# Attention sinks of eight heads turned and multiplied as one, and the inverse sums' transposes placed later

## The chip, the cores and the metric

The kernel runs on one core of a Trainium2 chip. The metric is device time in microseconds (us) of one execution, as the median of three runs. A core has five engines that work side by side, each through its own list of instructions in order: TensorE (PE in the profile; its weight loads are listed apart as PEld), VectorE (DVE), ScalarE (ACT), GpSimd (POOL) and SyncE (SP), which here only issues DMAs.

## The reference

Windowed attention with sinks is followed by two MoE-like layers:

```python
scores = scale * np.matmul(q, k.transpose(0, 1, 3, 2))      # q, k, v: 2 x 8 heads x 768 x 64
keep = (pos[None, :] < n_sink) | ((rel >= 0) & (rel < window))   # n_sink 4, window 128
a = softmax(np.where(keep, scores, -1e9))
x = np.matmul(a, v)                                          # -> 1536 tokens x 512
x = (g1(x @ w_in1)) @ w_out1                                 # 512 -> 2048 -> 512, g1(h) = h * tanh(softplus(h))
out = (g2(x @ w_in2)) @ w_out2                               # the same shape, g2(h) = h * clip(h + 3, 0, 6) / 6
```

The weights arrive as 64-bit numbers and are decoded on the chip.

## The kernel before, in words

The sequence of each of the two batches is cut into six units of 128 queries, with all eight heads in a unit. Eight units are computed early, in full float32, before and beside the first MoE matmuls: 6 and 7 (the second batch's first two) and 0 to 5 (the first batch), in the order 6, 7, 0, 1, 2, 3, 4, 5. The other four are computed later by other functions. Tokens go through the MoE in three blocks; the first block needs units 6, 7, 0 and 1, the second 2 to 5.

A query of a unit sees the keys of its own unit and of the one before. From the third unit of a batch on (i > 1, the early units 2 to 5) the sinks, keys 0 to 15, lie outside these, so each head has a third segment of 16 columns: scores are 128 x 272 a head (128 + 128 + 16). An early unit goes through these steps of the class `First`, where g is one of two halves of four heads:

- `prep`: keys and queries are turned by TensorE and copied by ScalarE; GpSimd puts the 16 sink keys behind the unit's keys (line 331).
- `scores(g)`: score matmuls (350), VectorE adds the mask and takes the extreme (354), ScalarE takes the exponential and its row sum (358).
- `turn(g)`: the exponentials `d` are transposed by TensorE (369) and copied to `at` by ScalarE or VectorE (371, 373). If i > 1, VectorE gathers the sink columns of four heads into `ds`, 128 x 64 (377), TensorE turns it (379), VectorE copies it to `ats`, 64 x 128 (380).
- `values(g)`: for i > 1 first one sink matmul for each pair of heads, over 64 rows, four heads by 16 sinks (388), and then the window's matmuls (393), all into the unit's one PSUM tile `o`.
- `inverse`: VectorE takes the reciprocal of the row sums (401, 402), GpSimd spreads it over 128 x 512 as `rb` (405), TensorE turns `rb` in four transposes (407), and ScalarE copies the result to `rib` (409).
- `normalise`: VectorE multiplies `o` by `rib` (413). `outputs` splits the product into two halves of 16 bits (419, 420).

`first_blocks` emits the steps of neighbouring units interleaved. The emission order is not quite the order of execution: a planner lays out the instructions of each engine by priority and by its own forecast of times, so that weight decoding (lines 210 to 224), emitted later, stands in gaps of VectorE and ScalarE. Transposes of attention and the MoE's accumulators share four PSUM banks (`ps_acc`), scores, `o` and the MoE's hidden layer four others (`ps_h`).

The sink values are laid out once for a batch in `first_sinks`: 16 sinks of each head are loaded as 64 rows for each half by two DMAs (303). GpSimd multiplies the rows by a column of `selh` for each of four head places (306), which leaves a block matrix `vsb`, so that one matmul adds each head's own sinks. `selh` is the sum of two column sets, `a` for rows 0 to 63 and `b_` for rows 64 to 127, made by VectorE (149 to 153).

The MoE stages are steps of an up-projection (lines 737 to 739) and a down-projection (782), the second one step behind. VectorE's line 754 makes the down-projection's input.

Of the kernel before, what the change touches and what calls it, by code (L numbers as in the profile page):

```python
# [7 lines left out]
F32 = mybir.dt.float32  # L8
# [4 lines left out]
ALU = mybir.AluOpType  # L13
# [16 lines left out]
def attention_moe_moe2(  # L30
# [13 lines left out]
    nc = tc.nc  # L44
    B, H, S, D = q.shape
# [6 lines left out]
    HP = H // 2  # L52
# [6 lines left out]
    const = main.enter_context(tc.tile_pool(name="const", bufs=1))  # L59
# [7 lines left out]
    ps_acc = main.enter_context(tc.tile_pool(name="ps_acc", bufs=4, space=PSUM))  # L67
# [20 lines left out]
    m1, m2 = m_all[:, 0:256], m_all[:, 128:400]  # L88
    m0 = const.tile([128, 128], F32)
    selh = const.tile([128, 4], F32)  # L90
    ident = const.tile([128, 128], F32)
    nsw = keep.tile([128, 2], F32)

# [28 lines left out]
    def emit_masks():  # L122
        ns, wd = nsw[:, 0:1], nsw[:, 1:2]
        tmp = part_p.tile([128, 4, 128], F32, tag="part", name="tmp")
        col, rel, ind, dg = (tmp[:, i] for i in range(4))
        nc.gpsimd.iota(col, pattern=[[1, 128]], base=0, channel_multiplier=0, allow_small_or_imprecise_dtypes=True)
        nc.gpsimd.iota(rel, pattern=[[-1, 128]], base=0, channel_multiplier=1, allow_small_or_imprecise_dtypes=True)
        nc.vector.tensor_scalar(out=ident, in0=rel, scalar1=0.0, scalar2=None, op0=ALU.is_equal)

        nc.vector.tensor_scalar(out=ind, in0=rel, scalar1=0.0, scalar2=None, op0=ALU.is_ge)  # L130
        nc.vector.scalar_tensor_tensor(out=dg, in0=rel, scalar=wd, in1=ind, op0=ALU.is_lt, op1=ALU.mult)
        nc.vector.tensor_scalar(out=m2[:, 0:128], in0=dg, scalar1=-BIG, scalar2=BIG, op0=ALU.mult, op1=ALU.add)

        nc.vector.scalar_tensor_tensor(out=ind, in0=col, scalar=ns, in1=dg, op0=ALU.is_lt, op1=ALU.max)
        nc.vector.tensor_scalar(out=m0, in0=ind, scalar1=-BIG, scalar2=BIG, op0=ALU.mult, op1=ALU.add)

        nc.vector.tensor_scalar(out=ind[:, 0:16], in0=col[:, 0:16], scalar1=ns, scalar2=None, op0=ALU.is_lt)
        nc.vector.tensor_scalar(out=m2[:, 256:272], in0=ind[:, 0:16], scalar1=-BIG, scalar2=BIG, op0=ALU.mult, op1=ALU.add)

        nc.vector.tensor_scalar(out=dg, in0=rel, scalar1=128.0, scalar2=wd, op0=ALU.add, op1=ALU.is_lt)  # L140
        nc.vector.tensor_scalar(out=m2[:, 128:256], in0=dg, scalar1=-BIG, scalar2=BIG, op0=ALU.mult, op1=ALU.add)
        nc.vector.scalar_tensor_tensor(out=ind, in0=col, scalar=ns, in1=dg, op0=ALU.is_lt, op1=ALU.max)
        nc.vector.tensor_scalar(out=m1[:, 0:128], in0=ind, scalar1=-BIG, scalar2=BIG, op0=ALU.mult, op1=ALU.add)

        hp = const.tile([128, 4], F32)
        nc.gpsimd.iota(hp, pattern=[[-16, 4]], base=0, channel_multiplier=1, allow_small_or_imprecise_dtypes=True)
        a = const.tile([128, 4], F32)
        b_ = const.tile([128, 4], F32)
        nc.vector.tensor_scalar(out=a, in0=hp, scalar1=0.0, scalar2=None, op0=ALU.is_ge)
        nc.vector.scalar_tensor_tensor(out=a, in0=hp, scalar=16.0, in1=a, op0=ALU.is_lt, op1=ALU.mult)  # L150
        nc.vector.tensor_scalar(out=b_, in0=hp, scalar1=64.0, scalar2=None, op0=ALU.is_ge)
        nc.vector.scalar_tensor_tensor(out=b_, in0=hp, scalar=80.0, in1=b_, op0=ALU.is_lt, op1=ALU.mult)
        nc.vector.tensor_tensor(out=selh, in0=a, in1=b_, op=ALU.add)
# [131 lines left out]
    sink_n = {}  # L285
# [10 lines left out]
    def first_sinks(b):  # L296


        ks1 = c_p.tile([128, HP, 16], F32, name=f"ks1_{b}")
        nc.scalar.activation(out=ks1, in_=kv_n[b * NSB][0][:, :, 0:16], func=AF.Copy)  # L300
        vsn = c_p.tile([64, 2, D], F32, name=f"vsn_{b}")
        for g in range(2):
            nc.sync.dma_start(out=vsn[:, g, :], in_=v[b, 4 * g:4 * g + 4, 0:16, :])
        vsb = c_p.tile([64, 2, 4, D], F32, name=f"vsb_{b}")
        for h in range(4):
            nc.gpsimd.tensor_scalar(out=vsb[:, :, h, :], in0=vsn, scalar1=selh[0:64, h:h + 1], scalar2=None, op0=ALU.mult)
        sink_n[b] = (ks1, vsb)

    class First:
        def __init__(self, u):  # L310
            self.u = u
            self.b, self.i = divmod(u, NSB)
            self.d, self.at, self.ats = [None, None], [None, None], [None, None]

        def prep(self, pin=False):
            u, b, i = self.u, self.b, self.i
# [46 lines left out]
        def turn(self, g):  # L363
            d = self.d[g]
            at = self.at[g] = v_p.tile([128, 2, 4, 128], F32, tag="at", name="at")
            for m in range(len(self.kvs)):
                tp = ps_acc.tile([128, 4, 128], F32, tag="acc", name="tp")
                for hh in range(4):
                    nc.tensor.transpose(tp[:, hh, :], d[:, hh, m * 128:(m + 1) * 128], ident)
                if m <= g:  # L370
                    nc.scalar.activation(out=at[:, m], in_=tp, func=AF.Copy)
                else:
                    nc.vector.tensor_copy(out=at[:, m], in_=tp)
            if self.i > 1:
                ats = self.ats[g] = s_p.tile([64, 128], F32, tag="ats", name="ats")
                ds = s_p.tile([128, 4, 16], F32, tag="ds", name="ds")
                nc.vector.tensor_copy(out=ds, in_=d[:, :, 256:272])
                tp = ps_acc.tile([64, 128], F32, tag="acc", name="tp")
                nc.tensor.transpose(tp, ds.rearrange("p h s -> p (h s)"), ident)
                nc.vector.tensor_copy(out=ats, in_=tp)  # L380

        def values(self, g):
            if g == 0:
                self.o = ps_h.tile([128, HP, 128], F32, tag="h", name="o")
            if self.i > 1:
                for c in (2 * g, 2 * g + 1):
                    vsb = sink_n[self.b][1][:, g, 2 * (c % 2):2 * (c % 2) + 2].rearrange("p h d -> p (h d)")
                    nc.tensor.matmul(self.o[:, c, :], vsb, self.ats[g], start=c == 0, stop=False, skip_group_check=True)
            for c in (2 * g, 2 * g + 1):
                for m, kv in enumerate(self.kvs):  # L390
                    for r in range(2):
                        h = 2 * c + r
                        nc.tensor.matmul(  # L393
                            self.o[64 * r:64 * r + 64, c, :], kv[1][:, h, :], self.at[g][:, m, h % 4, :],
                            start=self.i <= 1 and c == 0 and m == 0, stop=c == HP - 1 and m == len(self.kvs) - 1, skip_group_check=True,
                        )

        def inverse(self):
            rs = s_p.tile([128, H], F32, tag="rs", name="rs")
            ri = s_p.tile([128, H, 1], F32, tag="ri", name="ri")  # L400
            nc.vector.tensor_scalar(out=rs, in0=self.sums, scalar1=1e-9, scalar2=2.0 ** -SX, op0=ALU.add, op1=ALU.mult)
            nc.vector.reciprocal(out=ri[:, :, 0], in_=rs)
            tp = ps_acc.tile([128, HP, 128], F32, tag="acc", name="tp")
            rb = b_p.tile([128, H, D], F32, tag="rb", name="rb")
            nc.gpsimd.tensor_copy(out=rb, in_=ri.to_broadcast([128, H, D]))
            for c in range(HP):
                nc.tensor.transpose(tp[:, c, :], rb[:, 2 * c:2 * c + 2, :].rearrange("p a d -> p (a d)"), ident)
            self.rib = rib = b_p.tile([128, HP, 128], F32, tag="rib", name="rib")
            nc.scalar.activation(out=rib, in_=tp, func=AF.Copy)
# [14 lines left out]
    def first_blocks():  # L424
# [7 lines left out]
        for n, e in enumerate(us):  # L432
            f = us[n + 1] if n + 1 < len(us) else None
            if n + 4 < len(us):
                load_first(first[n + 4])
            e.turn(0)
            if f:
                f.scores(0)
            if f is None:
                next(moe)  # L440
            if n > 0:
                us[n - 1].outputs()
            e.values(0)
            if n + 2 < len(us):
                us[n + 2].prep()
            e.inverse()
            e.turn(1)
            if f:
                f.scores(1)
            if n == len(us) - 2:  # L450
                next(moe)
            e.values(1)
            e.normalise()
# [263 lines left out]
    acc = {}  # L717
# [504 lines left out]
```

## Time and profile before

| | |
|---|---|
| median of 3 runs | 600.29 us (599.73 to 600.51) |
| profiled execution | 599.53 us, of which the span of the instructions is 597.7 us |
| TensorE matmul busy | 579.0 us, 97% |
| TensorE weight loads busy | 394.4 us, 66% |
| VectorE busy | 457.8 us, 77% |
| ScalarE busy | 398.4 us, 67% |
| GpSimd busy | 24.8 us, 4% |

The busy time of an engine is the part of the span in which an instruction ran on it. The ends of matmuls are modelled and neighbouring ones overlap, so a busy TensorE can still be a waiting one. An average over the span also hides that stages have different limits; views of single stretches show these. A chain of work is followed back from the last instruction, at each step to what released it.

### The profile page before, as it was taken

The page shows a single profiled execution, that of the slowest core. Times are in us where ns is not written, and L with a number is a line of the kernel's source. Part 1 is how long each engine was busy: PE and PEld are TensorE (multiplying, and loading weights), DVE is VectorE, ACT ScalarE, POOL GpSimd, SP SyncE. Part 2 cuts the span into 40 slices and gives each one's busy share as a digit, 9 for nine tenths or more (in the row PEclk, how much of TensorE's full clock was granted, in tenths as well). Part 3 has the DMA queues.
Part 4 walks back from the last instruction along what each step waited for, and adds up shares of the span by engine and source line. Part 5 has one row for each costly group of instructions (what it writes and reads, how often), then busy time and mean ns, then how long its engine had stood idle before and what let it go on. Part 6 is the DMA issues. An engine that isn't in the chain of part 4 may idle for free.

```text
span 597.7 us, 11394 instructions
## 1 busy us (share of the span) xinstructions
PE 579.0 (97%) x4430; PEld 394.4 (66%) x4430; DVE 457.8 (77%) x1102; ACT 398.4 (67%) x786; POOL 24.8 (4%) x36
## 2 busy tenths in 40 slices
PE   7999999999999999899989999999999999999996
PEld 4778754444444545444434468888888888888885
DVE  5688998999365555489999999866687889874754
ACT  5998887777687776679888887434354656553532
POOL 0040010700000000000000000000000000000000
PEclk9999999999999999999999999999999999999999
DMA  9976357998334533254453442000007676400001
GB/s 179 226 163 212 101 183 199 230 261 213 96 73 74 80 60 73 47 159 141 157 192 122 163 143 71 1 1 2 1 7 249 215 263 223 142 34 1 36 1 39
DMA packets 105842, 72.24 MB, mean 121 GB/s; under 512 B 73512, under 2 KB 98088, under 8 KB 105784
## 3 DMA queue, kind: packets, MB, share of 16 engines
q1 hardware_dynamic: 105784, 71.48, 42.9%
q8 instruction: 35, 0.57, 0.4%
q14 instruction: 23, 0.19, 0.1%
HBM read 60.43 MB, written 3.15 MB: 106 GB/s over the span
## 4 chain that ended last, share of the span: by engine, by line
PE 59%; DVE 13%; ACT 12%; issue 11%; DMA 2%; POOL 2%; SPq 1%; DVEq 0%; ACTq 0%
PE acc L846 18%; PE h L806 7%; PE h L808 7%; PE h L807 7%; PE acc L782 6%; PE h L737 3%; PE h L739 2%; PE h L738 2%; DVE p L212 2%; ACT e L745 2%; ACT e L746 2%; DVE g L754 2%; ACT d L358 2%; ACT y L215 1%; PE o L393 1%
## 5 line engine op out<-in xcount | busy, mean ns | idle before, releaser
L782 PE MATMUL acc<-g,w 128*128 128x512 f16 x576 | 131.2, 379 | 5.4 <-DVE g L754 5.1
L846 PE MATMUL acc<-w,g 128*128 128x256 f16 x1008 | 113.8, 273 | 0.0
L846 PEld LDWEIGHTS <-g 128*128 128x128 f16 x1008 | 98.6, 98 | 11.4
L806 PE MATMUL h<-xt,w 128*128 128x256 f16 x384 | 104.7, 273 | 0.0
L808 PE MATMUL h<-xt,w 128*128 128x256 f16 x384 | 104.7, 273 | 0.0
L807 PE MATMUL h<-xt,w 128*128 128x256 f16 x384 | 104.7, 273 | 0.0
L782 PEld LDWEIGHTS <-w 128*128 128x128 f16 x576 | 55.3, 98 | 71.6 <-issue 7.0
L737 PE MATMUL h<-xt,w 128*128 128x512 f16 x192 | 72.8, 379 | 1.8 <-DVE mins L558 1.2
L739 PE MATMUL h<-xt,w 128*128 128x512 f16 x192 | 72.8, 379 | 0.0
L738 PE MATMUL h<-xt,w 128*128 128x512 f16 x192 | 72.8, 379 | 0.0
L810 ACT ACTIVATE e<-h,bias 128x512 f32<-128x512 f32 x48 | 32.5, 678 | 54.5 <-PE h L808 54.5
L811 DVE SCALAR_TENSOR_TENSOR e<-e,h 128x512 f32<-128x512 f32 x48 | 32.8, 684 | 41.8 <-ACT e L810 41.8
L823 ACT ACTIVATE g<-e 128x256 f16<-128x256 f32 x96 | 29.5, 354 | 28.8 <-DVE e L811 28.8
L823 ACT ACTIVATE g<-sm 128x512 f16<-128x512 f32 x48 | 30.2, 628 | 27.5 <-DVE sm L818 27.5
L749 DVE SCALAR_TENSOR_TENSOR e<-e,h 128x512 f32<-128x512 f32 x48 | 30.8, 683 | 16.5 <-ACT e L747 16.3
L824 DVE SCALAR_TENSOR_TENSOR g<-sm,g 128x512 f16<-128x512 f32 x48 | 33.1, 689 | 10.9 <-ACT g L823 10.8
L806 PEld LDWEIGHTS <-w 128*128 128x128 f16 x384 | 37.6, 98 | 4.6
L807 PEld LDWEIGHTS <-w 128*128 128x128 f16 x384 | 37.6, 98 | 4.5
L808 PEld LDWEIGHTS <-w 128*128 128x128 f16 x384 | 37.6, 98 | 4.3
L212 DVE SCALAR_TENSOR_TENSOR p<-raw,y 128x1024 int32<-128x1024 int32 x32 | 39.8, 1243 | 0.4
L740 ACT ACTIVATE e<-h 128x512 f32<-128x512 f32 x48 | 28.1, 588 | 16.4 <-PE h L739 16.4
L754 DVE SCALAR_TENSOR_TENSOR g<-e,g 128x1024 f16<-128x1024 f32 x24 | 29.4, 1226 | 8.3 <-ACT g L753 8.3
(172 smaller groups left out, 934.8 us busy)
## 6 DMA issues: line engine op xcount, KB each, us to landing
raw<-in_moe_w_in_dram SPq DMA_DIRECT2D x48, 512.0 KB, 4.2
raw<-in_moe_w_out_dram SPq DMA_DIRECT2D x48, 512.0 KB, 5.0
out_dram<-ob SPq DMA_DIRECT2D x12, 256.0 KB, 2.5
first<-in_k_dram SPq DMA_DIRECT2D x8, 256.0 KB, 4.8
first<-in_q_dram SPq DMA_DIRECT2D x8, 256.0 KB, 4.9
first<-in_v_dram SPq DMA_DIRECT2D x8, 256.0 KB, 3.1
nk<-in_k_dram SPq DMA_DIRECT2D x5, 256.0 KB, 5.1
nv<-in_v_dram SPq DMA_DIRECT2D x5, 256.0 KB
```

The lines of the kernel that those rows point to most:

```text
L212: nc.vector.scalar_tensor_tensor(out=p, in0=t[:, :, 1], scalar=3, in1=y, op0=ALU.logical_shift_left, op1=ALU.bitwise_xor)
L737: nc.tensor.matmul(o, wh, x[:, 0, c, :], start=c == 0, stop=False)
L738: nc.tensor.matmul(o, wh, x[:, 1, c, :], start=False, stop=False)
L739: nc.tensor.matmul(o, wl, x[:, 0, c, :], start=False, stop=c == KD - 1)
L754: nc.vector.scalar_tensor_tensor(out=gl, in0=e, scalar=sc, in1=gh, op0=ALU.mult, op1=ALU.subtract)
L782: nc.tensor.matmul(o, l_, r_, start=first and m == 0 and x == 0, stop=last and end and x == 2, skip_group_check=True)
L806: nc.tensor.matmul(o, wh, x[:, 0, c, :], start=c == 0, stop=False)
L807: nc.tensor.matmul(o, wh, x[:, 1, c, :], start=False, stop=False)
L808: nc.tensor.matmul(o, wl, x[:, 0, c, :], start=False, stop=c == KD - 1)
L823: nc.scalar.activation(out=g[:, 0, d_], in_=src, func=AF.Copy, scale=sc)
L824: nc.vector.scalar_tensor_tensor(out=g[:, 1, d_], in0=src, scalar=sc, in1=g[:, 0, d_], op0=ALU.mult, op1=ALU.subtract)
L846: nc.tensor.matmul(a[n // 2][:, n % 2], l_, r_, start=f == fa and m == 0 and n % 2 == 0 and x == 0, stop=ends and m == 1 and x == 2 and (n ...
```

## The change

The sinks of a unit are handled for all eight heads at once: both halves gather into one `ds` of 128 x 128, which is turned once, at the end of `turn(1)`, and copied once. The sink matmuls run over 128 rows (eight heads by 16 sinks) and come last in `values(1)`, behind the window's matmuls. The sink values are loaded as 128 rows by one DMA, and GpSimd builds the block matrix in eight operations with `sel8`, whose two halves are the former `a` and `b_`. `inverse` is split: the transposes and ScalarE's copy move into `spread`, emitted behind `turn(1)` instead of ahead of it.

```diff
+    sel8 = const.tile([128, H], F32)
...
-        a = const.tile([128, 4], F32)
-        b_ = const.tile([128, 4], F32)
+        a, b_ = sel8[:, 0:4], sel8[:, 4:8]
...
-        vsn = c_p.tile([64, 2, D], F32, name=f"vsn_{b}")
-        for g in range(2):
-            nc.sync.dma_start(out=vsn[:, g, :], in_=v[b, 4 * g:4 * g + 4, 0:16, :])
-        vsb = c_p.tile([64, 2, 4, D], F32, name=f"vsb_{b}")
-        for h in range(4):
-            nc.gpsimd.tensor_scalar(out=vsb[:, :, h, :], in0=vsn, scalar1=selh[0:64, h:h + 1], scalar2=None, op0=ALU.mult)
+        vsn = c_p.tile([128, D], F32, name=f"vsn_{b}")
+        nc.sync.dma_start(out=vsn, in_=v[b, :, 0:16, :])
+        vsb = c_p.tile([128, H, D], F32, name=f"vsb_{b}")
+        for h in range(H):
+            nc.gpsimd.tensor_scalar(out=vsb[:, h, :], in0=vsn, scalar1=sel8[:, h:h + 1], scalar2=None, op0=ALU.mult)
...
             if self.i > 1:
-                ats = self.ats[g] = s_p.tile([64, 128], F32, tag="ats", name="ats")
-                ds = s_p.tile([128, 4, 16], F32, tag="ds", name="ds")
-                nc.vector.tensor_copy(out=ds, in_=d[:, :, 256:272])
-                tp = ps_acc.tile([64, 128], F32, tag="acc", name="tp")
-                nc.tensor.transpose(tp, ds.rearrange("p h s -> p (h s)"), ident)
-                nc.vector.tensor_copy(out=ats, in_=tp)
+                if g == 0:
+                    self.ds = b_p.tile([128, H, 16], F32, tag="ds", name="ds")
+                nc.vector.tensor_copy(out=self.ds[:, 4 * g:4 * g + 4, :], in_=d[:, :, 256:272])
+                if g == 1:
+                    self.ats = b_p.tile([128, 128], F32, tag="ats", name="ats")
+                    tp = ps_acc.tile([128, 128], F32, tag="acc", name="tp")
+                    nc.tensor.transpose(tp, self.ds.rearrange("p h s -> p (h s)"), ident)
+                    nc.vector.tensor_copy(out=self.ats, in_=tp)
...
-            if self.i > 1:
-                for c in (2 * g, 2 * g + 1):
-                    vsb = sink_n[self.b][1][:, g, 2 * (c % 2):2 * (c % 2) + 2].rearrange("p h d -> p (h d)")
-                    nc.tensor.matmul(self.o[:, c, :], vsb, self.ats[g], start=c == 0, stop=False, skip_group_check=True)
...
+            if self.i > 1 and g == 1:
+                for c in range(HP):
+                    vsb = sink_n[self.b][1][:, 2 * c:2 * c + 2].rearrange("p h d -> p (h d)")
+                    nc.tensor.matmul(self.o[:, c, :], vsb, self.ats, start=False, stop=c == HP - 1, skip_group_check=True)
...
         def inverse(self):
...
+            self.rb = rb = b_p.tile([128, H, D], F32, tag="rb", name="rb")
+            nc.gpsimd.tensor_copy(out=rb, in_=ri.to_broadcast([128, H, D]))
+
+        def spread(self):
+            rb = self.rb
             tp = ps_acc.tile([128, HP, 128], F32, tag="acc", name="tp")
-            rb = b_p.tile([128, H, D], F32, tag="rb", name="rb")
-            nc.gpsimd.tensor_copy(out=rb, in_=ri.to_broadcast([128, H, D]))
             for c in range(HP):
                 nc.tensor.transpose(tp[:, c, :], rb[:, 2 * c:2 * c + 2, :].rearrange("p a d -> p (a d)"), ident)
...
             e.inverse()
             e.turn(1)
+            e.spread()
             if f:
                 f.scores(1)
```

## Rows read from the trace of the kernel before

**Rows 1.** Stretches: busy us (instructions) of PE, PEld, DVE, ACT, POOL; clock, DMA share, GB/s.
```profile
10.00:36.00 26.00, 24.21 (x241) 19.04 (x242) 19.02 (x81) 24.79 (x83) 7.63 (x11) 1.00 0.99 222
36.00:54.00 18.00, 17.20 (x183) 14.20 (x180) 14.61 (x51) 16.16 (x47) 1.42 (x3) 1.00 0.58 170
54.00:72.00 18.00, 16.86 (x173) 13.73 (x171) 17.77 (x56) 15.06 (x41) 1.67 (x2) 1.00 0.42 133
72.00:97.00 25.00, 25.00 (x162) 13.93 (x162) 23.68 (x37) 19.71 (x29) 1.57 (x1) 1.00 0.63 191
97.00:230.00 133.00, 129.61 (x830) 61.66 (x828) 91.51 (x171) 100.25 (x163) 11.83 (x12) 1.00 0.59 135
```
**Rows 2.** The chain that ended last, 36 to 97 us: start, us, what.
```profile
36.70 2.12 ACT d L358 x8
...
45.64 0.19 DVE ats L380
...
46.24 0.71 PE o L388 x4
...
59.14 1.07 POOL rb L405
...
60.25 0.67 PE tp L407 x4
...
60.94 0.60 ACT rib L409
61.54 0.98 ACT at L371 x2
...
80.45 0.11 PE tp L379
...
85.74 0.64 PE o L388 x4
```
**Rows 3.** Weight loads of TensorE in order of time, from 55 to 61 us.
```profile
55.95 0.52 PEld L388 LDWEIGHTS o<-ats,vsb 64*128 64x128 f32 x4 [0.34 <-DVE mins L354]
56.59 0.85 PEld L393 LDWEIGHTS o<-at,first 128*64 128x64 f32 x16
57.61 0.86 PEld L323 LDWEIGHTS tp<-ident,first 128*128 128x128 f32 x8 [0.17 <-issue]
58.63 0.76 PEld L350 LDWEIGHTS s<-kt,qt 64*128 64x128 f32 x10 [0.17 <-issue]
60.24 0.42 PEld L407 LDWEIGHTS tp<-ident,rb 128*128 128x128 f32 x4 [0.85 <-POOL rb L405]
60.63 0.91 PEld L369 LDWEIGHTS tp<-ident,d 128*128 128x128 f32 x8
```
**Rows 4.** Groups by shape, 0 to 96 us: busy, mean ns; idle before, releasers.
```profile
L388 PE MATMUL o<-ats,vsb 64*128 64x128 f32 x32 | 5.8, 297 | 0.5 <-DVE mins L354 0.3
...
L388 PEld LDWEIGHTS o<-ats,vsb 64*128 64x128 f32 x32 | 4.2, 186 | 2.6 <-DVE mins L354 1.1 <-issue 0.6 <-DVE p L212 0.4
...
L407 PEld LDWEIGHTS tp<-ident,rb 128*128 128x128 f32 x32 | 3.5, 141 | 1.9 <-POOL rb L405 1.5 <-issue 0.2
...
L380 DVE COPY ats<-tp 64x128 f32<-64x128 f32 x8 | 2.2, 275 | 1.0 <-PE tp L379 1.0
```
**Rows 5.** ScalarE's copy of the inverse and the product, unit 6, in order of time.
```profile
16.68 0.59 ACT L409 ACTIVATE rib<-tp 128x512 f32<-128x512 f32 x1
...
18.94 0.69 DVE L413 TENSOR_TENSOR xf<-o,rib 128x512 f32<-128x512 f32 x1 [0.49 <-PE o L393]
```
**Rows 6.** GpSimd and SP's queue in order of time, 28 to 40 us.
```profile
28.05 1.32 SPq L303 DMA_DIRECT2D vsn<-in_v_dram  x2
...
31.39 3.98 POOL L306 TENSOR_SCALAR vsb<-vsn,selh 64x128 f32<-64x128 f32 x4
...
39.70 0.62 POOL L405 COPY rb<-ri 128x512 f32<-128x512 f32 x1 [4.15 <-DVE ds L377]
```
**Rows 7.** TensorE's longest wait in total between 100 and 400 us.
```profile
PE acc L782 <- DVE g L754: 5.1, 6, 1.4
```

More of the change, by code (lines that the diff above doesn't have):

```diff
@@ L312, in __init__ @@
             self.b, self.i = divmod(u, NSB)
-            self.d, self.at, self.ats = [None, None], [None, None], [None, None]
+            self.d, self.at = [None, None], [None, None]
         def prep(self, pin=False):
@@ L394, in values @@
                             self.o[64 * r:64 * r + 64, c, :], kv[1][:, h, :], self.at[g][:, m, h % 4, :],
-                            start=self.i <= 1 and c == 0 and m == 0, stop=c == HP - 1 and m == len(self.kvs) - 1, skip_group_check=True,
+                            start=c == 0 and m == 0, stop=self.i <= 1 and c == HP - 1 and m == len(self.kvs) - 1, skip_group_check=True,
                         )
+            if self.i > 1 and g == 1:
+                for c in range(HP):
+                    vsb = sink_n[self.b][1][:, 2 * c:2 * c + 2].rearrange("p h d -> p (h d)")
+                    nc.tensor.matmul(self.o[:, c, :], vsb, self.ats, start=False, stop=c == HP - 1, skip_group_check=True)
         def inverse(self):
```

## The prediction, made before the kernel was run

> **What bounds the kernel now.** I read the busy time by stretches first [rows 1]. The change lives in the eight early attention units, which end at about 97 us, so the question is which engine is full there and whether time won there reaches the end. From 10 to 36 us ScalarE is full (24.79 of 26 us). From 36 to 54 us no engine is: TensorE's 17.20 of 18 us is a modelled figure, VectorE has 14.61, ScalarE 16.16. From 54 to 72 us VectorE is nearly full (17.77 of 18), because the decoding of the MoE weights fills it. From 72 us on the first MoE matmuls stand between the attention's, and TensorE shows no gap (25.00 of 25). From 97 to 230 us it stays so (129.61 of 133).
>
> Second, the chain that ended last [rows 2]. Between 36 and 72 us it changes engine all the time: exponentials on ScalarE, copies on VectorE, a little TensorE. One detour in it belongs to the change: VectorE's reciprocal, GpSimd's spread of it (1.07 us at 59.14), four transposes (0.67), ScalarE's copy (0.60), and only then the copies of the turned scores. After 72 us the chain is nearly all TensorE.
>
> Third, TensorE's weight loads in order of time [rows 3], which show the pace of a small matmul as the distance from one group's start to the next. Fourth, the groups by shape [rows 4] for the unit costs.
>
> **The change part by part.** It touches two things: the sinks in the four units that have a separate sink segment (units 2 to 5 of the first batch), and the place of the inverse sums' four transposes in all eight units.
>
> *Sink matmuls.* Before, each of the four units multiplies its sinks in two groups over 64 rows, ahead of the window's matmuls; after, in one group over 128 rows, behind them. The number of records stays at 32 (four bytes wide, two records each) [rows 4]. Before, a group of four starts at 55.95 and the next group at 56.59 [rows 3]: 0.64 us, 0.16 us a record. The nearest row of the new shape, 128 rows by 128 columns, is the inverse sums' group: four from 60.24 to 60.63, 0.39 us or 0.10 us a record [rows 3]; I use 0.107 (eight in 0.86 us), because eight more transposes of this shape right behind need 0.91 us of loads. A unit goes from 1.28 to 0.86 us, 0.42 us less, 1.7 us over four. The bounds are 0.16 (nothing saved) and 0.10 us a record (1.9 us). I take 0.107, since it is the same shape.
>
> The weight load of 64 rows takes 186 ns and that of 128 rows 141 ns [rows 4]. The Trainium skill (TensorE: Matmul & The Clock Gate, section on LDWEIGHTS) says that the time of a weight load follows the columns and not the rows, so by it the loads of 64 and of 128 rows cost the same; the time that this would give is the third rival's. The rows here disagree with it, and no run so far shows why.
>
> *Sink transposes.* Eight of 64 columns become four of 128. On the chain one takes 0.11 us, at 80.45 [rows 2]. Four fewer are 0.4 us of TensorE.
>
> *Copies on VectorE.* The two gathers a unit stay, with the same elements. The copies of turned sinks (275 ns, 0.19 us on the chain) go from eight to four, since 128 partitions cost what 64 do by free size. Three of the eight stand on the chain between 36 and 72 us, all in the first half of a unit, which is the half that loses its copy: 3 x 0.19 = 0.57 us.
>
> *Waits ahead of the sinks.* The loads of the old sink matmuls stood idle for 2.6 us [rows 4], mostly behind VectorE. As first matmul into the unit's PSUM tile they also carried the wait for its bank, which now passes to the window's first matmul. I count nothing for it; the most it can give is the 2.6 us. The new wait, sinks for the one turned copy, comes after the next unit's scores and the window's matmuls (16 records, over 0.85 us of loads [rows 3]), more than the copy's 0.275 us. If that cover were gone, it would cost that 0.275 us in each of four units, 1.1 us.
>
> *The later inverse transposes.* TensorE executes in order, so four transposes waiting for GpSimd hold up the turning of the second half, whose inputs are ready earlier. Loads were idle 1.5 us for that, in two places [rows 4]. The larger: the scores before it began at 58.63 with 0.76 us of loads, so TensorE was free at 59.39 or, with the last matmul running out, 59.6; the turn began at 60.63 [rows 3]. Turned first, it starts about 1.1 us sooner, and ScalarE's copies with it, since they stood behind the inverse's copy [rows 2]. That is 1.1 us on the chain; bounds 0.66 and 1.5. The smaller one is in a stretch where ScalarE had other work ahead of the copy: I count nothing. In the first four units ScalarE is full [rows 1], and an exchange of two of its copies wins nothing.
>
> What is late next: the copy of the inverse sums moves back by two copies of turned scores (0.98 us [rows 2]) and is then covered by the second half's values. In the tightest unit it ended at 17.27 and the product that needs it began at 18.94 [rows 5], 1.67 us of cover. Each us beyond that would be paid on VectorE.
>
> *Building the sink matrix.* On GpSimd four operations become eight, each on half the elements per partition. Four took 3.98 us [rows 6]; eight take 4.0 us if they go by elements and 8.0 if by count. GpSimd's next work that somebody waits for is at 39.70 [rows 6]; from 31.39 that leaves 8.3 us, so even the upper bound is hidden, and the matrix itself is wanted later than before. One DMA of 128 rows takes the place of two that occupied SP's queue for 1.32 us [rows 6]; behind them wait loads of later units. At most 0.7 us of queue is freed; the loads behind are for units that start several us later, so I count nothing. The selector columns on VectorE are written into one tile instead of two, with no more work.
>
> *The sum.* Between 36 and 72 us: 1.1 for the detour, 0.57 for copies, 0.42 for the matmuls of the one unit whose sinks are on the chain as TensorE work (46.24 [rows 2]); together 2.1 us. After 72 us, where everything on TensorE counts: the last unit's two groups 1.28 to 0.86, the unit before gets its whole sinks there (0.64 to 0.86), two transposes less (0.2): 0.4 us. Sum 2.5 us. Against the profiled execution (599.53 us; span 597.7 and 1.8 around it) that is 597.0. The median of the three timed runs is 0.76 above the profiled one, so the forecast is 600.29 - 2.5 = 597.8 us.
>
> It reaches the end because TensorE has few gaps from 72 to 230 us, and the work behind is released by it: an earlier start moves the whole train. What eats of it is VectorE: TensorE waited 5.1 us in all for the product of line 754 between 100 and 400 us [rows 7], behind decoding in VectorE's order.
>
> **The rivals.** *Larger gain.* All matmul savings (1.7), transposes (0.4), waits for GpSimd (1.5) and half of the idle before the sinks (1.3) count: 4.9 us, 595.4. For it: TensorE is the only engine whose work falls much. Against: from 54 to 72 us VectorE is full, and the chain rests on TensorE for a quarter of that time only.
>
> *VectorE keeps the gain.* If VectorE sets the pace from 54 us into the first MoE stage, the gain is its own saving: four copies of 0.19 to 0.275 us, 0.8 to 1.1 us. That gives 599.3. For it: 17.77 of 18 and 23.68 of 25 us [rows 1], and the waits on line 754. Against: the detour lies in front of VectorE's work too, and from 97 to 230 us VectorE has 91.5 of 133 us.
>
> *The wider matmul is no cheaper.* If a record of 128 rows takes the 0.16 us of the 64-row one, the unit on the chain saves nothing, the last unit nothing, and the unit before it pays 0.64 us more after 72 us; with 0.2 us for transposes, 1.1 for the detour and 0.57 for copies the gain is 1.2 us, 599.1. For it: the idle before the loads was behind other engines, and part of the 0.64 us may be such a wait. Against: every group of 128 rows in the trace goes at 0.11 us or less. The rule on weight loads cited above would have it so.
>
> *The inverse copy comes too late (slower).* The planner orders the instructions of an engine by its own forecast. If it puts ScalarE's four exponentials of the next unit (2.12 us for four with their reads [rows 2]) ahead of the inverse's copy, the copy is late by 0.98 + 2.12 = 3.1 us, 1.4 more than the tightest cover and less than that in the next three; VectorE then waits with everything behind the product, and the PSUM bank is kept. About 1.2 us in each of three or four units is some 4 us, less the 2.5 won: 601.8. It decides from a delay of 1.67 us. For it: the exponentials release VectorE's work. Against: at three of the four places the cover is larger.
>
> **How the numbers follow.** Forecast 0.40, larger gain 0.12, VectorE keeps it 0.22, matmul no cheaper 0.12, slower 0.14. A change of 0.2%, 1.2 us, is about what the measurement can tell. The first two cases are faster, half of the matmul case, and a fifth of VectorE's; together 0.62. Same 0.24, slower 0.14. The range goes from the larger gain (595.4) to a little over no change (600.8), which leaves out most of the slower case; the likeliest case's own range is 596.3 to 599.0.
>
> **What would show it.** Right: the turn of the second half stands ahead of the inverse transposes, no matmul of these waits for GpSimd, sink groups of eight records in about 0.86 us, and the first MoE matmul about 2 us sooner with all later ones. Wrong: line 413's product waiting for ScalarE's copy; new waits before the sinks; an earlier MoE start that is lost to waits on line 754 by 230 us.

## The result and the profile after

The changed kernel measured 603.55 us (601.41 to 604.57, nine runs) beside 600.01 us of the kernel before: ratio 1.0059, 95% interval 1.0046 to 1.0072. It is slower by 3.5 us, where 2.5 us less was forecast, and lies above the forecast's range. About 2 us of this go with a lower TensorE clock, which seven of its nine executions had (last section). The profiled execution took 603.33 us with a span of 601.5 us, 3.8 us over the span of before.

First the stretches of the kernel after, columns as in [rows 1]; the last two rows are cut out of the fourth one.

```profile
36.00:54.00 18.00, 17.35 (x179) 14.54 (x177) 15.25 (x49) 16.50 (x47) 2.44 (x4) 1.00 0.59 165
54.00:72.00 18.00, 16.44 (x169) 13.61 (x170) 17.13 (x50) 14.23 (x39) 2.01 (x2) 1.00 0.39 126
72.00:97.00 25.00, 25.00 (x159) 14.03 (x159) 24.53 (x39) 19.94 (x31) 1.50 (x1) 1.00 0.61 190
97.00:230.00 133.00, 126.69 (x781) 59.45 (x779) 88.63 (x164) 97.13 (x158) 9.80 (x12) 0.99 0.58 135
...
145.00:150.00 5.00, 2.61 (x8) 0.83 (x7) 5.00 (x7) 4.93 (x7) 0.00 (x0) 0.79 0.85 216
150.00:155.00 5.00, 5.00 (x21) 2.11 (x20) 2.59 (x4) 2.45 (x3) 0.00 (x0) 0.87 0.49 106
```

Up to 72 us TensorE has a little less to do than before, from 72 to 97 us it is full in both, and the loss is in the row from 97 to 230 us: TensorE is busy for 126.69 us instead of 129.61 [rows 1], so it stood for 2.9 us more. Where in it, is shown by the starts of VectorE's product that makes the input of the down-projection (line 754 before, 759 after):

| product no. | 1 | 2 | 3 | 4 | 5 | 6 | 7 | 8 | 9 | 14 |
|---|---|---|---|---|---|---|---|---|---|---|
| before, us | 86.64 | 94.51 | 111.34 | 120.46 | 132.31 | 144.69 | 154.71 | 162.85 | 177.10 | 239.89 |
| after, us | 85.33 | 93.22 | 111.39 | 121.46 | 134.07 | 147.14 | 153.93 | 166.71 | 180.95 | 243.74 |
| difference | -1.31 | -1.29 | +0.05 | +1.00 | +1.76 | +2.45 | -0.78 | +3.86 | +3.85 | +3.85 |

The early part did win: 1.3 us by 93 us. Between 93 and 167 us 5.1 us are lost, and from there both kernels run alike. The seventh product came sooner after the change, but TensorE reached the matmuls that use it only at 159.75 us (155.89 before), so nothing was won by it. (The first product of `xf`, line 413 before and 417 after, starts between 18.62 and 19.27 us in the traces. Counted from it to the eighth, the early units take 72.86 us after and 73.83 before, so the early gain proper is 1.0 us.)

The early gain is first seen in the second unit. Its product waited 2.27 us for TensorE before (first line) and waits 0.61 us now (second line):

```profile
27.93 0.69 DVE L413 TENSOR_TENSOR xf<-o,rib 128x512 f32<-128x512 f32 x1 [2.27 <-PE o L393]
...
26.56 0.69 DVE L417 TENSOR_TENSOR xf<-o,rib 128x512 f32<-128x512 f32 x1 [0.61 <-PE o L390]
```

The early part of the kernel after: the chain that ended last, and then the weight loads of TensorE in order of time.

```profile
51.98 1.09 PE o L397 x8
...
58.88 0.63 PE tp L411 x4
...
90.28 1.09 PE o L397 x8
```

```profile
51.91 0.97 PEld L397 LDWEIGHTS o<-ats,vsb 128*128 128x128 f32 x8 [0.17 <-issue]
52.80 0.91 PEld L368 LDWEIGHTS tp<-ident,d 128*128 128x128 f32 x8
...
55.62 0.88 PEld L390 LDWEIGHTS o<-at,first 128*64 128x64 f32 x16 [0.76 <-issue]
...
57.50 0.91 PEld L368 LDWEIGHTS tp<-ident,d 128*128 128x128 f32 x8
...
58.85 0.42 PEld L411 LDWEIGHTS tp<-ident,rb 128*128 128x128 f32 x4 [0.34 <-issue]
```

The turn of the second half (57.50) now stands ahead of the inverse's transposes (58.85), and the 0.85 us behind GpSimd [rows 3] is gone. A group of eight sink records takes 0.89 us (51.91 to 52.80). But all of these groups are on the chain now, 1.09 us each, and the window's first matmul, which follows no sinks any more, still waits (0.76 us at 55.62).

The groups by shape of the kernel after, 0 to 96 us, and the product of line 417 over 36 to 97 us:

```profile
L305 POOL TENSOR_SCALAR vsb<-vsn,sel 128x64 f32<-128x64 f32 x8 | 4.8, 623 | 1.4 <-DMA vsn<-in_v_dram 1.4
L397 PEld LDWEIGHTS o<-ats,vsb 128*128 128x128 f32 x32 | 3.9, 191 | 0.7 <-issue 0.7
L411 PEld LDWEIGHTS tp<-ident,rb 128*128 128x128 f32 x32 | 3.5, 140 | 1.5 <-POOL rb L405 0.8 <-issue 0.7
L381 DVE COPY ats<-tp 128x128 f32<-128x128 f32 x4 | 1.1, 280 | 0.4 <-PE tp L380 0.4
...
L417 DVE TENSOR_TENSOR xf<-o,rib 128x512 f32<-128x512 f32 x5 | 3.4, 689 | 0.9 <-PE o L397 0.7 <-ACT w L222 0.2
```

The product shows no wait for `rib`; it waits for the sinks' matmuls, which it did not before.

Now the place of the loss. VectorE and then SyncE's queue of the kernel after, in order of time:

```profile
109.54 0.78 DVE L508 SCALAR_TENSOR_TENSOR k<-nk,k 128x512 f16<-128x512 f32 x1 [0.26 <-ACT k L507]
...
115.93 0.75 DVE L210 TENSOR_SCALAR y<-raw 128x1024 int16<-128x1024 int16 x1 [2.63 <-DMA raw<-in_moe_w_out_dram]
```

```profile
110.35 1.31 SPq L510 DMA_TRANSPOSE kt<-k  x1
111.72 0.57 SPq L170 DMA_DIRECT2D raw<-in_moe_w_out_dram  x1
```

VectorE's decoding waits 2.63 us for a load of w_out that SyncE issues at 111.72 us. It stands in SyncE's queue behind a DMA transpose of `kt`, a late attention unit's keys, which waits for VectorE's `k`, done at 110.3 us. In the kernel before, SyncE issued this load at 109.88 us, another of w_in behind it, and the transpose only at 113.28 us; VectorE waited 0.82 us. None of these lines is in the change; the order of both queues is the planner's.

TensorE's weight loads behind it, and then its longest wait in total, 100 to 400 us, which was 5.1 us in [rows 7]:

```profile
112.75 4.63 PEld L787 LDWEIGHTS <-w 128*128 128x128 f16 x22 [1.80 <-issue]
...
146.02 0.10 PEld L787 LDWEIGHTS <-w 128*128 128x128 f16 x1 [0.65 <-issue]
148.41 0.10 PEld L787 LDWEIGHTS <-w 128*128 128x128 f16 x1 [2.30 <-issue]
148.79 0.15 PEld L787 LDWEIGHTS <-w 128*128 128x128 f16 x1 [0.28 <-issue]
...
151.34 3.12 PEld L787 LDWEIGHTS <-w 128*128 128x128 f16 x15 [0.26 <-issue]
```

```profile
PE acc L787 <- DVE g L759: 7.2, 6, 2.0
```

### The profile page after: what moved, and what is told of

The parts are those of the page before. It is cut to its first block, busy times and chain, and to the rows that moved or that the text cites. A ratio compares the mean times of both kernels' runs of the same rounds, so it can differ in the third digit from the quotient of the medians.

```text
span 601.5 us, 11388 instructions
## 1 busy us (share of the span) xinstructions
PE 579.3 (96%) x4426; PEld 395.1 (66%) x4426; DVE 458.8 (76%) x1098; ACT 397.9 (66%) x786; POOL 24.1 (4%) x40
## 4 chain that ended last, share of the span: by engine, by line
PE 63%; issue 12%; ACT 11%; DVE 9%; DMA 2%; POOL 1%; SPq 1%; POOLq 0%; DVEq 0%; ACTq 0%
PE acc L851 18%; PE acc L787 7%; PE h L811 7%; PE h L812 7%; PE h L813 7%; PE h L742 3%; PE h L744 2%; PE h L743 2%; PE o L390 2%; PE s L349 2%; ACT e L750 2%; ACT e L751 2%; PE tp L368 2%; DVE g L759 1%; DVE p L212 1%
```

## The experiments

The kernel before ran beside each set of experiments at 599.78 to 599.95 us. In most of them the order of the MoE instructions on some engines is held, in that each is made to follow the one ahead of it in a given list; this sets the order of issue and adds no wait between engines. A list covers about 97 to 150 us where nothing else is said; over it the two kernels' orders differ on SyncE (in 14 places), VectorE (28) and ScalarE (12).

```diff
+ORDER = {"SP": [...], "DVE": [...], "Activation": [...]}     # numbers of MoE instructions
...
+    for a, b in zip(order, order[1:]):
+        tc.add_manual_dep(mine[b], mine[a].name, kind, reason="order")
```

**The whole order, both ways.** The changed kernel with the order of before on the three engines:

> The changed kernel with its attention as it is, and with VectorE's, ScalarE's and SP's instructions between about 97 and 150 us put into the order that they had in the kernel before. Order theory (the planner's new order of weight decoding, late attention and weight loads costs the 5 us between 93 and 158 us): the 1.3 us won up to 93 us stay, 598.7 us, between 597.5 and 599.6, no half clock near 148 us. Timing rival (an earlier end of the early attention makes transfers and decoding collide whatever their order): 602.5 to 604.

Measured 598.75 us, ratio 0.9984 (0.9975 to 0.9993). And the kernel before with the changed kernel's order:

> The kernel before with the order of the changed one on the same three engines between about 97 and 150 us, attention untouched. Order theory: it loses the 5.2 us that the changed kernel lost after 93 us without having won 1.3 us before, 604 to 605.5, with waits for line 754's product of over 1.5 us and a stretch at half clock near 148 us. Timing rival: 600, as before.

Measured 604.72 us, ratio 1.0085 (1.0067 to 1.0103). The order alone costs 4.8 us in the changed kernel and 4.9 us in the kernel before, and the change without it wins 1.1 us. The half clock that was expected with it did not come in the profiled execution of the second run; more of that below.

**Which engine's order.** Only SyncE held:

> The changed kernel, in which only SyncE's queue is held in the order of the kernel before over the stretch of about 97 to 150 us; VectorE and ScalarE keep the changed kernel's own order. Holding all three gave 598.75, holding none 603.55, so 4.8 us are to be shared out. Theory (both orders cost, each by its own wait): the late load of w_out costs the 1.8 us that VectorE's wait for it grew (0.82 to 2.63 us), the rest, about 3 us, is VectorE's order; expected 601.8 us, and VectorE's wait for w_out near 112 us back under 1 us. Rival (VectorE's order alone): the wait for w_out only fills time that VectorE's queue would lose anyway, 603.3 us. Second rival (the transfer alone): 598.8 us.

Measured 599.31 us (0.9989; 0.9980 to 0.9998): the second rival, nearly. Only VectorE and ScalarE held:

> The counterpart: VectorE and ScalarE are held in the order of the kernel before over that stretch, SyncE's queue keeps the changed kernel's own order, in which the DMA transpose of kt stands ahead of the load of w_out. Theory (both orders cost): 598.8 + 1.8 = 600.6 us. Rival (VectorE's order alone): 598.8 us. Second rival (the transfer alone): 603.4 us.

Measured 598.60 us (0.9981; 0.9972 to 0.9990). It tells nothing on the question: SyncE's order, left to the planner, came out as in the kernel before but for one load of keys near 130 us, so this is the first experiment again. So the missing corner was made with SyncE held in the new order too, in both kernels, and TensorE's MoE matmuls held in the order that the kernels share:

> The changed kernel with SyncE's queue held in the changed kernel's own order, and VectorE and ScalarE held in the order of the kernel before (about 97 to 150 us; TensorE's order as in the changed kernel). The run before it that was meant for this did not hold SyncE, whose order then came out as in the kernel before. Theory (SyncE's order alone costs the time: the other way round, with VectorE's new and SyncE's old order, 599.31 were measured): 598.75 + 4.2 = 603 us. Rival (only both together cost it: VectorE's old order has work ahead of the late load that covers the wait): 599 to 600 us.

> The kernel before, in which nothing is changed but SyncE's order over about 97 to 150 us, taken from the changed kernel; VectorE, ScalarE and TensorE are held as they were. Theory (SyncE's order alone): 604 us, near the 604.72 that all three new orders gave in this kernel. Rival (only both together): 600 to 601 us.

Measured 607.92 us (1.0135; 1.0121 to 1.0150) and 607.99 us (1.0144; 1.0128 to 1.0160), beyond both theories. The table for the changed kernel:

| | VectorE, ScalarE old | new |
|---|---|---|
| SyncE old | 598.75 | 599.31 |
| SyncE new | 607.92 | 603.55 |

SyncE's order is the cause; VectorE's new order softens it. (In the corner of 599.31 us VectorE and ScalarE were left to the planner and kept the new order up to about 133 us only.) Rows of two corners show how. First SyncE old, VectorE new: SyncE's queue, and VectorE's decoding.

```profile
107.65 0.55 SPq L170 DMA_DIRECT2D raw<-in_moe_w_out_dram  x1
...
110.87 1.31 SPq L510 DMA_TRANSPOSE kt<-k  x1
...
113.90 0.76 DVE L210 TENSOR_SCALAR y<-raw 128x1024 int16<-128x1024 int16 x1
```

Then SyncE new, VectorE old:

```profile
112.88 1.31 SPq L510 DMA_TRANSPOSE kt<-k  x1
114.24 0.57 SPq L170 DMA_DIRECT2D raw<-in_moe_w_out_dram  x1
...
112.14 0.68 DVE L508 SCALAR_TENSOR_TENSOR k<-nk,k 128x512 f16<-128x512 f32 x1
...
118.43 0.75 DVE L210 TENSOR_SCALAR y<-raw 128x1024 int16<-128x1024 int16 x1 [4.78 <-DMA raw<-in_moe_w_out_dram]
```

The load can't be issued before the transpose ahead of it, and that one not before VectorE's `k`. With the transpose behind the loads, w_out is issued at 107.65 us and VectorE's decoding does not wait for it; with the transpose ahead, it is issued 1.4 us after `k` is ready, wherever VectorE has put `k`: wait 2.63 us with `k` started at 109.54, 4.78 us with `k` at 112.14.

**Which place in SyncE's queue.** All orders of the changed kernel held, but the transpose near 110 us put back behind the weight loads that it had overtaken (two, w_out and w_in; the expectations say three by mistake); and the counterpart, old order only behind 115 us.

```diff
-"SP": [... 31, 30, 32, 33, ..., 50, 51, 43, 44, 52, ...]   # the changed kernel; 30 is the transpose of kt
+"SP": [... 31, 32, 33, 30, ..., 50, 51, 43, 44, 52, ...]   # first place as before
+"SP": [... 31, 30, 32, 33, ..., 50, 51, 52, 43, 44, ...]   # second place as before
```

> The changed kernel with all its own orders held, but at one place of SyncE's queue, near 110 us: the DMA transpose of kt goes back behind the three weight loads that it had overtaken, as in the kernel before. Theory (this one place makes VectorE wait 2.63 us for w_out at 113 us, and every later loss follows): 599.3 us, as with SyncE's whole old order. Rival (the second place, between about 120 and 145 us, where two loads of w_in and w_out overtake loads of nk and nv, costs the second half): 601.4 us.

> The counterpart: SyncE's order goes back to that of the kernel before only behind about 115 us, and the transpose of kt near 110 us stays ahead of the three weight loads. Theory (the first place alone): 603.3 us, as the changed kernel. Rival (both places cost half each): 601.4 us.

Measured 600.63 us (1.0020; 1.0004 to 1.0036) and 603.51 us (1.0049; 1.0036 to 1.0062). Mending the first place gives back 2.9 us, mending only the second nothing. With SyncE's whole old order 1.3 us more came back (599.31), but that these are the second place's is not shown: VectorE's and ScalarE's orders differ there too from about 133 us on, and in the profiled executions the run with the first place mended was already behind at the fourth product (120.79 and 119.45 us), ahead of the second place.

**The two parts of the change, alone.** Only the inverse's transposes later, without and with the old order held:

```diff
             e.inverse()
             e.turn(1)
+            e.spread()
```

> Only the inverse sums' transposes are moved behind the turn of the second half; sinks as before. By the prediction's step it wins 1.1 us at the one place where TensorE waited for GpSimd, so the first MoE product comes about 1 us sooner; the end is then 599 us if the order behind stays, and up to 604 if the planner's order behind it is as unlucky as the changed kernel's. Rival: the later copy of the inverse delays line 413's product, and the first MoE product comes no sooner.

> The kernel before with only the inverse sums' transposes emitted later, and the order of the MoE instructions of about 97 to 150 us held as in the kernel before on SyncE, VectorE and ScalarE. Without the held order it measured 601.44 us, and its last attention unit ended 0.34 us sooner than before (counted from its first). Theory (with the order held, the end moves by what the early units win): 599.86 - 0.3 = 599.5 us. Rival (the detour behind GpSimd is worth what the prediction gave it, 1.1 us, and the early rows understate it): 598.7 us. Rival (the later transposes cost by themselves, not by the order): 601.4 us again.

Measured 601.44 us (1.0020; 1.0009 to 1.0031) and 599.23 us (0.9993; 0.9983 to 1.0003). By itself the planner gave this kernel a worse order too, worth 2.2 us; with the order held the part wins 0.7 us at the median, which the interval does not tell from nothing. Only the sinks, in the same two ways:

> Only the sinks of eight heads in one; the inverse sums' transposes as before. By the prediction's steps 1.4 us are won (copies 0.57, matmuls and transposes 0.82), so 598.6 us if the order behind stays. If a matmul over 128 rows is no cheaper, 0.6 us at most. If the planner changes the order behind, the end says little and the first MoE product's time is to be read instead.

> The kernel before with only the sinks of all eight heads in one transpose and last, the inverse sums' transposes in their old place, and the order of the MoE instructions of about 97 to 150 us held as in the kernel before. Without the held order it measured 600.49 us, and its last attention unit ended 1.41 us later than before (counted from its first). Theory (the sinks alone lose 1.4 us in the early units, and with the order held the end moves by that): 601.2 us. Rival (parts add: the pair with the order held won 1.1 us, the later transposes alone 0.3, so the sinks alone 0.8): 599.1 us.

Measured 600.49 us (1.0008; 1.0000 to 1.0017) and 600.40 us (1.0013; 1.0004 to 1.0022). The sinks' part alone loses: in the second of these the early units take 75.25 us instead of 73.83, and 0.5 us of it are left at the end. VectorE's product and TensorE's loads ahead of it there:

```profile
64.58 0.97 PEld L397 LDWEIGHTS o<-ats,vsb 128*128 128x128 f32 x8 [0.17 <-issue]
...
65.78 0.69 DVE L414 TENSOR_TENSOR xf<-o,rib 128x512 f32<-128x512 f32 x1 [0.83 <-PE o L397]
```

**What a group of sinks costs at either place.** Two kernels with sink matmuls left out, the order of before held:

```diff
-            if self.i > 1:                        # kernel before, values(g)
+            if self.i > 1 and g == 1:             # no sinks in the first half
...
-            if self.i > 1 and g == 1:             # changed kernel, values(g)
+            if False:                             # no sink matmuls
```

> The kernel before with its order of about 97 to 150 us held, and the sink matmuls of each unit's first half left out (16 of 32 records; copies and transposes of the sinks stay), so that part of the sinks is missing from the result. Theory (these groups, ahead of the window's matmuls, fill a wait that the window has anyway: its first matmul started 2.52 us after the product of xf before and 2.51 us after it in the changed kernel, which has no such group): not over 0.5 us won, 599.4 to 600 us. Rival (they stand on the path, as the prediction priced them, 0.64 us in the unit on the chain and 0.64 in the last): 598.6 us.

> The changed kernel with the order of the kernel before held at about 97 to 150 us, as in the run that measured 598.75, and the sink matmuls left out altogether (32 records, groups of 0.89 us at the end of four units), so that the sinks' values are missing from the result. Theory (at the end of the unit the group stands on the path to the product of xf, which waited for its last matmul in three units, 0.44, 0.30 and 0.83 us in rows of VectorE): 1.5 to 3 us won, 596.0 to 597.3 us. Rival (the group is covered there too, by VectorE's decoding): under 0.5 us, 598.3 to 598.8 us.

Counted to the eighth product of `xf`, the theory seems to hold for the first: without the four first-half groups of before the early units took 73.80 us instead of 73.83. The rows ahead of it say otherwise. The sixth and seventh products came 1.0 and 1.1 us sooner (45.18 and 59.82 us behind the first; 46.19 and 60.91 before), and in one unit the window's first matmul came 0.65 us sooner (55.94 instead of 56.59 us). The last unit lost the gain, because more MoE matmuls stood ahead of its last twelve. TensorE's loads there, first of the kernel before, then without the first-half groups:

```profile
90.18 0.55 PEld L782 LDWEIGHTS <-w 128*128 128x128 f16 x4
91.15 0.20 PEld L393 LDWEIGHTS o<-at,first 128*64 128x64 f32 x4 [0.42 <-ACT at L371]
91.52 0.10 PEld L782 LDWEIGHTS <-w 128*128 128x128 f16 x1 [0.17 <-issue]
91.84 0.64 PEld L393 LDWEIGHTS o<-at,first 128*64 128x64 f32 x12 [0.23 <-issue]
```

```profile
89.00 0.55 PEld L782 LDWEIGHTS <-w 128*128 128x128 f16 x4
89.97 0.20 PEld L393 LDWEIGHTS o<-at,first 128*64 128x64 f32 x4 [0.42 <-ACT at L371]
90.33 0.98 PEld L782 LDWEIGHTS <-w 128*128 128x128 f16 x6 [0.17 <-issue]
91.74 0.64 PEld L393 LDWEIGHTS o<-at,first 128*64 128x64 f32 x12 [0.42 <-ACT at L371]
```

In all, 62 MoE matmuls ran ahead of these twelve instead of 56; at 0.216 us each that is 1.3 us, by estimate what the four groups, 4 x 0.64 us of TensorE, had really cost. So they were about half covered, not free.

Without the four groups of the changed kernel the early units took 68.51 us instead of 73.00, with 53 MoE matmuls ahead in both: 4.5 us, about 1.1 a group, at least the whole group. But at the end both kernels, which do less work, were slower: 602.97 us (1.0044; 1.0030 to 1.0058) and 605.09 us (1.0085; 1.0071 to 1.0098). The first was 1.4 us behind at the third product (112.78 and 111.34 us); its chain there runs through a load of `nv` of 5.49 us, and no run was made on it. In the second, VectorE, ScalarE and TensorE's loads:

```profile
99.83 0.69 DVE L508 SCALAR_TENSOR_TENSOR k<-nk,k 128x512 f16<-128x512 f32 x1 [4.22 <-ACT k L507]
...
98.13 1.15 ACT L751 ACTIVATE e<-e,fifth 128x1024 f32<-128x1024 f32 x1
99.18 0.61 ACT L507 ACTIVATE k<-nk 128x512 f16<-128x512 f32 x1
...
110.74 0.10 PEld L743 LDWEIGHTS <-w 128*128 128x128 f16 x1 [5.18 <-issue]
```

Again an order: ScalarE's copy of `k`, just ahead of the stretch that was held, went behind two passes of the MoE's activation (the second is shown), and TensorE stood for 5.18 us at 105.5. So the old order was held from the first MoE instruction on:

> As the run before, the changed kernel with all sink matmuls left out (the sinks' values are missing from the result), but with the order of the kernel before held for the MoE instructions of SyncE, VectorE and ScalarE from their first one to about 150 us, not from about 97 us on. In the run before, the last early product came 4.85 us sooner than in the kernel with its sinks, and VectorE then waited 4.22 us for a copy of k that ScalarE had put behind two exponentials. Theory (the order is what an early gain is lost to; with all of it held the gain reaches the end): 594 to 596 us. Rival (loads and the other engines set the time from 100 us on, whatever the order): 598 to 599 us.

> The changed kernel, complete, with the same longer stretch of the old order held (from the first MoE instruction to about 150 us). It is the comparison for the run without sinks. Theory: as with the shorter stretch, 598.7 us. Rival (the planner's new early order was part of the early gain of about 1 us, and the old one gives it back): 599.7 us.

Measured 599.35 us and 599.45 us (both 1.0000; 0.9987 to 1.0013). The first came out near its rival, the second as its rival had it. Without sinks the early units ended 4.0 us sooner than in the comparison (70.06 and 74.08 us), the third of VectorE's products of the table above came 1.3 us sooner (109.71 and 110.97), the eighth 1.5 us (161.61 and 163.11), and behind 150 us, where no order was held, the rest went. The stretches of the kernel without sinks, columns as above:

```profile
72.00:87.00 15.00, 14.77 (x96) 8.08 (x95) 14.60 (x22) 11.87 (x16) 0.94 (x1) 1.00 0.63 209
87.00:97.00 10.00, 10.00 (x56) 4.76 (x57) 9.67 (x17) 7.15 (x10) 0.00 (x0) 1.00 0.65 164
```

VectorE is full (24.27 of 25 us), and with an attention that ends 4 us sooner its first MoE product came only 0.9 us sooner (86.27 and 87.20). The comparison shows that the early gain needs the planner's new early order: with the old one the changed kernel's early units take 74.08 us, no less than before, and the end is at 599.45 us, not to be told from the kernel before. (The 598.75 with the shorter list is 0.7 us less, and the two intervals overlap.)

## Why the prediction was wrong

**The step that failed** is "it reaches the end": "TensorE has few gaps from 72 to 230 us, and the work behind is released by it: an earlier start moves the whole train". The argument took the order of the work behind as fixed. It was not: SyncE's queue came out in another order, and the order turned a gain of 1.1 us into a loss of 3.5 (shown from both kernels); the transpose ahead of the w_out load is 2.9 us of that. And even with the order held the train does not move one for one, and VectorE is full up to 97 us: 4.0 us won early by leaving out the sinks were 1.5 us at the eighth product and about nothing at the end. VectorE's row was there to read [rows 1]; TensorE's 25.00 of 25 us, a figure of the kind that the prediction itself calls modelled, was given the greater weight. The prediction had named what came as its last sign of being wrong: the start of the MoE was 1.3 us earlier, and it was lost to waits on line 754 (759 after; 7.2 us in all instead of 5.1).

**The slower rival** named the right mechanism, an order that the planner sets by its forecast, and the wrong queue. ScalarE's copy of the inverse never held up line 413's product. The prediction looked at SyncE's queue only near the two loads that the change merges; it was reordered some 80 us behind them, in work of other functions. *VectorE keeps the gain* fits VectorE's rows in the kernel without sinks, but it was not what decided.

**The terms.** *The detour behind GpSimd* (1.1 us): the turn stands first and the loads' waits for GpSimd fell from 1.5 to 0.8 us, but at its place nothing was won: with the later transposes alone the unit took 11.12 us from the fifth to the sixth product, 11.06 before. They won 1.05 us in the second unit (7.94 us instead of 8.99 from the first product to the second), where the prediction had ScalarE full and counted nothing, and 0.4 us were left by the eighth (73.43 instead of 73.83).

*The sink matmuls* (0.42 us won in the unit on the chain, 0.4 after 72 us, with the transposes): the new group's pace was right, 0.89 us for 0.86 predicted, and its place was not. At the end of the unit it costs all of its time, and the first-half groups that it replaces had cost only about half of theirs by the estimate above. "I count nothing for it" on the window's wait left out the same thing: in the changed kernel the window still waited (2.51 us behind the product of `xf`, 2.52 before), now with no sinks in the wait. The sinks alone lost 1.4 us by the eighth product. How much the second-half groups of before had cost was not measured, so these 1.4 us are not added up from parts.

*The copies* (0.57 us): there are four less, and no experiment parts them from the rest.

All terms together: 2.5 us forecast, 1.0 measured by 92 us, and that with the planner's early order. Why the parts make -0.4 and +1.4 alone and -1.0 together is open. Part of it may be MoE matmuls that change places with the last unit, as in the run without first-half groups; no run holds TensorE's early order to show it.

**The wider matmul.** A record costs 0.11 us, as forecast, and the third rival is out. The Trainium skill (TensorE: Matmul & The Clock Gate, section on LDWEIGHTS) says that a weight load goes by columns and not by rows; the rows after agree: 191 ns over 128 rows, 186 over 64 [rows 4]. The prediction had set a matmul's load beside a transpose's (140 ns, at equal rows and columns), and that difference is of another kind. The load's time does not set the pace of a group, however, so no time hung on it.

**GpSimd and the DMA.** Eight operations took 4.80 us within the bounds of 4.0 and 8.0, with 2.5 us to spare before GpSimd's next work: hidden, as said.

## What to carry to other kernels

Where a planner orders the queues, a change also changes the order of work that it doesn't touch. Compare the orders of each queue before reading any time, DMA queues first, and hold the old order to see what the edit itself is worth. Here the order behind 97 us was worth +4.8 us and the rest -1.1 us; with the old order held from the first MoE instruction on, the edit was worth nothing that could be measured. A transfer that waits for a result delayed the loads behind it in SyncE's queue; put loads that wait for nothing ahead of it.

Work that stands in front of a wait may cost less than its busy time, and the same work behind the wait all of it: leave it out and look before pricing its removal. And compare what else ran up to the point where you read the time: here six matmuls of another stage hid a gain of about 1.3 us.

## What the runs showed of the hardware

After the wait of 2.30 us the matmuls from 148.41 to 151.2 us started about every 0.43 us instead of every 0.216, and the granted clock of the stretch was 0.79, of the next 0.87, and 0.50 from 148 to 151 us: TensorE ran there at the lower of its two levels, 1.2 instead of 2.4 GHz, and seven matmuls took 1.4 us more. The same wait at the same place in the kernel with the first place mended had no such effect; TensorE's loads there:

```profile
145.81 0.10 PEld L787 LDWEIGHTS <-w 128*128 128x128 f16 x1 [0.20 <-issue]
148.21 4.63 PEld L787 LDWEIGHTS <-w 128*128 128x128 f16 x22 [2.30 <-issue]
```

22 loads in 4.63 us are the full pace. The wait of the single load ahead of it was 0.65 us there and is 0.20 here. Nor did the profiled execution of the kernel before with the new order show it (1.00 throughout 145 to 155 us, after waits of 1.34 and 1.87 us), and at 603.81 us it lost 4 us all the same. So a loss does not need the lower clock. Longer waits had it in other traces: 0.66 from 145 to 150 us after waits of 2.73 and 3.07 us in the two kernels with only SyncE's order new, and 0.54 from 110 to 115 us after the 5.18 us in the kernel without any sink matmuls that measured 605.09 us.

In the changed kernel the clock is part of the loss, and it differs between executions of the same program: two of the nine had a granted clock of 0.997 and 0.998 over the whole and took 601.41 and 601.76 us, the other seven 0.994 to 0.996 and 603.20 to 604.57 us. So in the comparisons above some 2 us of a time can be the clock's. What brings the clock down after one such wait and not after another is open.
